# Retention followed by an MLP mixer on one core: masks that read two PSUM banks, seven quarter products for a third of batch 0, two crossbar turns, and order tables

## The chip, the core and the metric

The kernel runs on one core of a Trainium2 chip. TensorE (PE) multiplies matrices and puts the result in PSUM, which has eight banks here; VectorE (DVE) and ScalarE (ACT) read PSUM and SBUF and write either; GpSimd (POOL) and SyncE (SP) mostly issue transfers here, and the crossbar transposes go over SP's queue. Each engine works through its own list of instructions in order, and semaphores order the lists against one another. The metric is the device time in microseconds of one execution.

## What is computed

The first half is a retention (a linear attention whose state decays by a factor gamma of the head), the second a token and channel mixing MLP on its result. Sizes are B = 4 batches, H = 8 heads, S = 768 positions, D = 64; the mixer has 512 channels, 256 token features and 1536 channel features.

```
gamma = 1.0 - 2.0 ** (-5.0 - np.arange(H))
for t in range(S):
    state = gamma * state + outer(k[:, :, t], v[:, :, t])
    y[:, :, t] = q[:, :, t] @ state / sqrt(D)
x = y.transpose(0, 2, 1, 3).reshape(B, S, H * D)
h = relu(x.T @ w_tok1) @ w_tok2
u = x + h.T
out = u + relu(u @ w_ch1) @ w_ch2
```

## The kernel before

Line numbers are those of the kernel before. Inputs are cast to f16 and products are summed in f32 in PSUM.

`front(b, p)` does retention and token mixing for a pair p of heads of batch b, 16 pairs in all. The 768 positions are six chunks of 128. Keys and queries are scaled by powers of gamma (`decayed`, L577 and L579), and each is turned so that the 64 dimensions of both heads lie on the partitions (`turn`): by PE transposes (L610 and L612) with a copy out of PSUM (L621, L626), or by the crossbar over SP's queue (L598). `TURNS` gives a letter for k, q and u of each pair: t and w are turned by PE, x by the crossbar. In batches 0 and 1 the letters are "twt", in batches 2 and 3 "xxx". Then come the scores (`sc`, L700), 12 products of 128x128 for both heads and six chunks into four banks, two for each half of the sequence (one for each head); the masks (`am`, L707), four DVE instructions of 128x384 that multiply a bank by the causal mask into SBUF; the products with v (`av`, L728) into two banks Y; the state of each chunk (`st`, L649, with the copy `u0` at L659 and the links of the recurrence at L665), its scaled copy (L675, L677) and its product with the turned q (`y2`, L738) into the same Y. Copies take x out of Y (L750), `t1` (L764) and `t2` (L785) are the token mixing, again in two halves over the two banks Y, and further copies take u and X out (L750 as well). u is turned by PE transposes (`tru`, L824, with the copy at L830) or by the crossbar (L813).

`back(b)` does the channel mixing. The wide step multiplies u by w_ch1, 512 to 1536 channels: `widen` (L859) in plain products for batch 0, and `widen7` for the other three batches (L932), which cuts u and the weights into quarters and needs seven products of quarters in place of eight. That costs differences of u (`ts`, L904) and of the weights (`asum`, L1174), intermediate copies (`keep` and `seed`, L885), and an addition with relu on DVE (`joined`, L953) for two of the four results. A block `i` of `widen7` yields the row tiles i and i + 6 of the 12. The narrow step is `narrow7` (L1057), with sums of h (`sm`, L1035), the weights' differences `wsum` (L1161) and additions into X (L1071). `store` writes the result.

The order is planned when the program is built. `ORDERED` is a string of operation numbers and `WAYS` says for operations that DVE or ACT can do which of them does it. `arrange` goes through them with a model of each engine and of the DMA queues (`Rings`), and gives each PSUM use the bank that comes free first. Each such use is a tile of its own, named by its bank:

```
slot.tile = ps.tile(shape, dtype, name=f"bank{slot.at}", bufs=1)
```

In the opening, products of zeros (L1205) fill places where PE would stand.

Of the kernel before, what the change touches and what calls it, by code (L numbers as in the profile page):

```python
# [15 lines left out]

class Slot:


    def __init__(self, tag, good=0, need=0):  # L20
        self.tag, self.users, self.tile, self.at = tag, [], None, None
        self.good, self.need = good, need
# [3 lines left out]

# [16 lines left out]
class Rings:  # L43

    GEN = dict(SP=20.0, POOL=8.0, ACT=20.0)
    FIRST = dict(SP=600, POOL=1800, ACT=700)
    OPENING = dict(SP=1300, POOL=3000, ACT=700)
    LAND = dict(SP=900, ACT=900)  # L50
    DT = 40.0
    EARLY = 10000
    SOFT = (0.48, 0.52)
    HARD = (0.52, 0.43)
    LATER = (1400, 200)
    LATE = 100000
    PL = (1800, 2400, 2700)
    PT = (13500, 27000)

    def __init__(self):  # L60
        self.t = 0.0
        self.line = dict(SP=[], POOL=[], ACT=[])
        self.made = dict(SP=[0.0, 0.0, 0.0], POOL=[0.0, 0.0, 0.0], ACT=[0.0, 0.0, 0.0])

    def land(self, q, op, t):
        if q == "POOL":
            return self.PL[(t >= self.PT[0]) + (t >= self.PT[1])]
        return self.LAND[q] + (self.LATER[t >= self.LATE] if op.dma[0] == 48 else 0)

    def add(self, q, op, start):  # L70
        first = max(start + (self.OPENING if len(self.made[q]) == 3 else self.FIRST)[q], self.made[q][-1])
        end = first + op.dma[0] * self.GEN[q]
        self.made[q].append(end)
        self.line[q].append([op, float(op.dma[0]), first, end])

    def busy(self):
        return any(self.line.values())

    def step(self, landed):
        dt, t = self.DT, self.t  # L80
        on = [(q, l[0]) for q, l in self.line.items() if l and l[0][2] <= t]
        if on:
            hard = len(on) - ("POOL" in dict(on))
            late = t >= self.EARLY
            for q, x in on:
                share = (self.SOFT[late] if hard else 1.0) if q == "POOL" else (self.HARD[late] if hard < len(on) else 1.0) / hard
                n = share * dt / x[0].dma[1]
                if x[3] > t:
                    n = min(n, dt / self.GEN[q])
                x[1] -= n  # L90
                if x[1] <= 0:
                    self.line[q].pop(0)
                    landed.append((x[0], t + dt + self.land(q, x[0], t)))
        self.t = t + dt


SEM = 80
F_ON = 21000
FILL, F_NS, F_COLD = 0.7, 218, 320
BLOCK, ASKED, NEEDED, PE_0 = 256, -80, 192, 2  # L100
FETCH = (8200, 5000, 95000)
ENGINES = ("PE", "ACT", "DVE", "POOL", "SP")
SWITCH = {("", "wide"): 92, ("", "high"): 92, ("wide", ""): 100, ("high", ""): 111, ("wide", "high"): 105,
          ("high", "wide"): 105}
FREE = dict(PE=300, ACT=1150, DVE=1090, POOL=1200, SP=750)


def arrange(ops, BUFS, BANKS, seq, ways):


    INF = 1e18
    n = len(ops)
    end, start, eng = [None] * n, [None] * n, [None] * n
    begun = [False] * n
    rings = Rings()
    free = dict(FREE)
    bank_slot = {i: None for i in range(8)}
    buf_slot = {t: [None] * m for t, m in BUFS.items()}
    lanes, turns = [], []
    line = {e: [] for e in ENGINES}  # L120
    for i in seq:
        line[ops[i].ways[ways[i]][0]].append(ops[i])
    at = dict.fromkeys(ENGINES, 0)
    order = []
    landed = []
    tiled = ""
    count, pe_at, fetched = PE_0, 1100, {}
    t = 0.0

    def slot_free(s):  # L130
        m = 0
        for u in s.users:
            x = end[u.n]
            if x is None:
                return INF
            if x > m:
                m = x
        return m + SEM

    def ready(o, e):  # L140
        m = 0
        if o.behind is not None and not begun[o.behind.n]:
            return INF
        for d in o.after:
            x = end[d.n]
            if x is None:
                return INF
            if x > m:
                m = x
        for d in o.deps:  # L150
            if not begun[d.n]:
                return INF
            if end[d.n] is None:
                return INF
            if eng[d.n] == e and e == "PE":
                x = start[d.n]
            else:
                x = end[d.n] + (25 if eng[d.n] == e and d.dma is None else SEM) + o.guard
            if x > m:
                m = x  # L160
        return m

    def room(o):
        m, got = 0, []
        for s in o.takes:
            best = None
            held = bank_slot if s.tag in BANKS else buf_slot[s.tag]
            for i in BANKS[s.tag] if s.tag in BANKS else range(BUFS[s.tag]):
                if any(g[1] == i and (g[0].tag in BANKS if s.tag in BANKS else g[0].tag == s.tag) for g in got):
                    continue  # L170
                if s.tag in BANKS and i == 7 and t < F_ON:
                    continue
                if s.need and (held[i] is None or held[i].good < s.need):
                    continue
                x = 0 if held[i] is None else slot_free(held[i])
                if best is None or x < best[0]:
                    best = (x, i)
            if best is None or best[0] >= INF:
                return INF, None
            got.append((s, best[1]))  # L180
            m = max(m, best[0])
        return m, got

    def lane(o, e):
        if o.dma is None or e == "POOL" or len(lanes) < 8:
            return 0
        x = end[lanes[-8].n]
        if x is None:
            return INF
        x += SEM  # L190
        if o.dma[0] == 48 and len(turns) > 2:
            y = end[turns[-3].n]
            if y is None:
                return INF
            x = max(x, y - 900)
        return x

    left = n
    while left:
        moved = False  # L200
        wake = INF
        for e in ENGINES:
            if free[e] > t:
                wake = min(wake, free[e])
                continue
            if at[e] >= len(line[e]):
                continue
            o = line[e][at[e]]
            r = ready(o, e)
            if r > t:  # L210
                wake = min(wake, r)
                continue
            m, banks = room(o)
            m = max(m, lane(o, e))
            if m > t:
                wake = min(wake, m)
                continue
            at[e] += 1
            way = o.ways[ways[o.n]]
            s_ = t  # L220
            if e == "PE":
                if o.tiled != tiled:
                    s_ = max(t, free[e] + SWITCH[tiled, o.tiled])
                tiled = o.tiled
                o.fill = int((s_ - pe_at) * FILL / (F_NS if pe_at > 2000 else F_COLD)) if s_ < F_ON and s_ - pe_at > 400 else 0
                count += 2 * o.fill
                o.busy = way[1]
                for x in range(count - 2 * o.fill, count + o.ins):
                    if (x - ASKED) % BLOCK == 0:
                        fetched[(x - ASKED) // BLOCK] = s_ + max(0, x - count) * o.busy / o.ins + FETCH[s_ > FETCH[2]]  # L230
                    if (x - NEEDED) % BLOCK == 0 and x > NEEDED:
                        late = fetched.get((x - NEEDED) // BLOCK, 0) - (s_ + max(0, x - count) * o.busy / o.ins)
                        o.busy += max(0, late)
                count += o.ins
                pe_at = s_ + o.busy
            else:
                o.busy = way[1]
            start[o.n], eng[o.n], begun[o.n] = s_, e, True
            free[e] = s_ + o.busy
            if o.dma:  # L240
                rings.add(e, o, t)
                if e != "POOL":
                    lanes.append(o)
                    if o.dma[0] == 48:
                        turns.append(o)
                if e == "SP":
                    free[e] = max(t + way[1], rings.made["SP"][-3])
# [989 lines left out]
```

## Time and profile before

| | |
|---|---|
| median of 3 runs | 186.33 us (186.3 to 188.1) |
| span of the profiled execution (its time is not listed apart) | 185.2 us |
| PE clock granted in every stretch of the trace | 1.00 |
| DMA moved | 25.31 MB, mean 137 GB/s |
| masks (L707) | 64 instructions, 32.1 us of DVE |
| longest single wait of PE (L612, for the scaled k) | 1.7 us |

The rows of the profile stand with the prediction. A row of the groups reads: line, engine, operation, what it writes and from what, partitions x elements, count | busy us in all, mean ns of one | idle time of the engine just before them and what ended most of it. A row of the waits reads: engine and line, what it waited for: us in all, times, longest. A row of the chain reads: start, length, engine, tile and line. A DMA row ends with the median us from issue to landing.

### The profile page before, as it was taken

The page shows a single profiled execution, that of the slowest core. Times are in us where ns is not written, and L with a number is a line of the kernel's source. Part 1 is how long each engine was busy: PE and PEld are TensorE (multiplying, and loading weights), DVE is VectorE, ACT ScalarE, POOL GpSimd, SP SyncE. Part 2 cuts the span into 40 slices and gives each one's busy share as a digit, 9 for nine tenths or more (in the row PEclk, how much of TensorE's full clock was granted, in tenths as well). Part 3 has the DMA queues.
Part 4 walks back from the last instruction along what each step waited for, and adds up shares of the span by engine and source line. Part 5 has one row for each costly group of instructions (what it writes and reads, how often), then busy time and mean ns, then how long its engine had stood idle before and what let it go on. Part 6 is the DMA issues. An engine that isn't in the chain of part 4 may idle for free.

```text
span 185.2 us, 5235 instructions
## 1 busy us (share of the span) xinstructions
PE 176.4 (95%) x2077; PEld 133.9 (72%) x2077; DVE 166.9 (90%) x423; ACT 128.8 (70%) x299; POOL 52.7 (28%) x63
## 2 busy tenths in 40 slices
PE   7688999999999999999999999999999999999991
PEld 2345788666788998877568988966678986667881
DVE  3599989969999999998999999999999799779982
ACT  4587797594797998899997778798673425754220
POOL 7986548375363218540604000000000000000000
PEclk9999999999999999999999999999999999999999
DMA  5999999999999999999999989225132162510054
GB/s 179 195 153 179 182 199 207 174 182 207 161 157 154 93 157 100 156 153 125 168 134 107 155 182 244 72 42 108 23 113 48 57 212 100 186 57 2 4 202 140
DMA packets 92393, 25.31 MB, mean 137 GB/s; under 512 B 82000, under 2 KB 89552, under 8 KB 92368
## 3 DMA queue, kind: packets, MB, share of 16 engines
q0 software_dynamic: 67184, 12.78, 91.1%
q1 hardware_dynamic: 23600, 9.70, 25.9%
q10 hardware_dynamic: 1584, 2.49, 3.8%
q8 instruction: 16, 0.26, 0.6%
q14 instruction: 9, 0.07, 0.1%
HBM read 26.74 MB, written 6.29 MB: 178 GB/s over the span
## 4 chain that ended last, share of the span: by engine, by line
PE 85%; DVE 7%; DMA 4%; ACT 1%; SPq 0%; issue 0%; DVEq 0%; ACTq 0%
PE bank L1057 30%; PE bank L932 22%; PE bank L859 9%; PE bank L764 6%; PE bank L785 5%; DVE am L707 4%; DMA us<-in_k_dram 4%; PE bank L700 3%; PE bank L728 3%; PE bank L738 2%; PE bank L649 2%; PE bank L824 1%; DVE U L665 1%; DVE qT L621 1%; PE bank L612 1%; PE bank L610 1%
## 5 line engine op out<-in xcount | busy, mean ns | idle before, releaser
L707 DVE TENSOR_TENSOR am<-bank,mask 128x384 f16<-128x384 f32 x64 | 32.1, 546 | 0.4 <-PE bank L700 0.2
L885 ACT COPY us<-bank 128x384 f32<-128x384 f32 (+1 forms) x47 | 20.0, 434 | 16.5 <-PE bank L1057 14.0
L1057 PEld LDWEIGHTS <-hs 128*128 128x128 f16 x282 | 26.5, 98 | 3.6 <-DVE hs L1035 0.3
L880 ACT ACTIVATE h<-bank 128x384 f16<-128x384 f32 x49 | 23.4, 498 | 7.5 <-PE bank L859 3.9
L1057 PE MATMUL bank<-wsum,hs 128*128 128x256 f16 x216 | 27.9, 273 | 0.0
L932 PE MATMUL bank<-hs,late 128*128 128x384 f16 x108 | 23.3, 326 | 0.0
L1057 PEld LDWEIGHTS <-h 128*128 128x128 f16 x216 | 20.5, 98 | 3.0
L523 POOL DMA_DIRECT2D v<-in_v_dram x16 | 16.3, 1020 | 22.3 <-PE bank L728 12.2
L953 DVE CUSTOM_DVE_ANT_0 h<-bank,us 128x384 f16<-128x384 f32 x36 | 19.1, 550 | 2.3 <-PE bank L932 2.2
L1071 DVE TENSOR_TENSOR X<-X,bank 128x256 f32<-128x256 f32 (+1 forms) x49 | 19.3, 405 | 1.1 <-PE bank L1057 0.7
L1057 PE MATMUL bank<-wc,h 128*128 128x256 f16 x144 | 19.2, 273 | 0.0
L932 PEld LDWEIGHTS <-late 128*128 128x128 f16 x144 | 13.3, 98 | 7.8
L859 PE MATMUL bank<-uT,wc 128*128 128x384 f16 x96 | 17.9, 326 | 0.0
L523 POOL DMA_DIRECT2D k<-in_k_dram x15 | 15.4, 1031 | 7.7 <-ACT cross L675 2.0
L675 ACT ACTIVATE cross<-U,gp 64x320 f16<-64x320 f32 x27 | 15.1, 558 | 3.2 <-DVE U L665 2.9
L665 DVE SCALAR_TENSOR_TENSOR U<-U,gp,bank 128x64 f32<-128x64 f32 x64 | 16.8, 271 | 0.6
L885 ACT COPY bank<-bank 128x384 f32<-128x384 f32 (+1 forms) x28 | 12.1, 436 | 5.8 <-PE bank L932 3.4
L932 PE MATMUL bank<-uT,wc 128*128 128x384 f16 x72 | 15.8, 326 | 0.0
L785 PE MATMUL bank<-h,wt 128*128 128x128 f16 x192 | 14.3, 219 | 0.0
L750 ACT CAST x<-bank 128x384 f16<-128x384 f32 x27 | 12.2, 485 | 2.9 <-PE bank L738 2.6
L750 ACT COPY X<-bank 128x384 f32<-128x384 f32 x26 | 12.5, 493 | 1.8 <-PE bank L785 1.6
L932 PEld LDWEIGHTS <-wc 128*128 128x128 f16 x108 | 9.9, 98 | 5.1
(93 smaller groups left out, 342.6 us busy)
## 6 DMA issues: line engine op xcount, KB each, us to landing
out_dram<-X SPq DMA_DIRECT2D x13, 256.0 KB, 2.6
v<-in_v_dram POOLq DMA_DIRECT2D x16, 192.0 KB, 8.4
k<-in_k_dram POOLq DMA_DIRECT2D x15, 192.0 KB, 10.0
q<-in_q_dram POOLq DMA_DIRECT2D x14, 192.0 KB, 8.7
wc<-in_moe_w_ch_dram POOLq DMA_DIRECT2D x5, 512.0 KB, 13.1
out_dram<-X ACTq DMA_DIRECT2D x9, 256.0 KB, 2.1
hs<-in_q_dram SPq DMA_DIRECT2D x2, 384.0 KB, 3.6
wc<-in_moe_w_ch_dram POOLq DMA_DIRECT2D x2, 256.0 KB, 9.6
```

The lines of the kernel that those rows point to most:

```text
L523: (nc.sync if hard else nc.gpsimd).dma_start(out=tile_of(s, [P, 2, NC, D], FP if hard else F16), in_=src.rearrange("h (c p) d -> p (h c) d ...
L665: nc.vector.scalar_tensor_tensor(out=u[:, c], in0=u[:, c - 1], scalar=gp[:, p:p + 1], in1=chunk(c), op0=ALU.mult, op1=ALU.add)
L707: nc.vector.tensor_tensor(am, SC[g].tile[:, :m * P].rearrange("p (i t) -> p i t", t=P), (mask2[:, g // 2:g // 2 + 1] if paired else mask). ...
L750: (nc.scalar.copy if e == "ACT" else nc.vector.tensor_copy)(tile(), t)
L785: nc.tensor.matmul(Y[j].tile[:, 2 * i * D:2 * (i + 1) * D], wt2[:, jt, t], H1.tile[:, jt], start=False, stop=(jt == NJ - 1), skip_group_ch ...
L859: nc.tensor.matmul(acc[:, :SH], wc1[:, ct, ft * P:(ft + 1) * P], UT.tile[:, ct, sh * SH:(sh + 1) * SH], start=(ct == 0), stop=(ct == NP - 1))
L880: nc.scalar.activation(out, src, AF.Relu)
L885: (nc.scalar.copy if e == "ACT" else nc.vector.tensor_copy)(out, src)
L932: nc.tensor.matmul(acc[:, :SH], left(ct), r[:, ct], start=first and ct == 0, stop=ct == C2 - 1, skip_group_check=True)
L953: nc.vector._custom_dve(TENSOR_ADD_SAT, out=h(m, sh), in0=R.tile[:, :SH], in1=KS.tile[:, j], s0=BIG, s1=0.0)
L1057: nc.tensor.matmul(acc[:, lo], l[:, j], r[:, j], start=first and j == 0, stop=j == K2 - 1, skip_group_check=True)
L1071: nc.vector.tensor_tensor(dst(), dst(), b_(), ALU.add)
```

## The change

PSUM becomes one tile of eight banks. A slot is a slice of it; where two banks are to be read by one instruction, `two` takes them as one view with a stride:

```diff
+    psum = ps.tile([P, 8, 512], FP, name="psum")
...
-            slot.tile = ps.tile(shape, dtype, name=f"bank{slot.at}", bufs=1)
+            slot.tile = psum[:, slot.at]
+            if dtype != FP:
+                slot.tile = slot.tile.bitcast(dtype)
...
+    def two(a, b):
+        lo, hi = sorted((a.at, b.at))
+        both = psum[:, lo:hi + 1:hi - lo]
+        a.tile, b.tile = both[:, 0], both[:, 1]
+        return both
```

The masks take both heads of a half of the sequence at once: two instructions of 128x768 for a pair in place of four of 128x384. The buffers of their results are four of the double size in place of eight. `av` waits for one mask where it waited for two.

```diff
+        for hf in range(2):
+            def emit(hf=hf):
+                am = tile_of(AM[hf], [P, 2, HC, P], F16)
+                nc.vector.tensor_tensor(am, pairs[hf][:, :, :SH].rearrange("p j (i t) -> p j i t", t=P),
+                                        mask.unsqueeze(1).to_broadcast([P, 2, HC, P]), ALU.mult)
+            am_ops.append(op(one("DVE", dve(2 * SH), emit), [sc, mask_op], [AM[hf]], SC[2 * hf:2 * hf + 2], key="am"))
```

In batch 0, row tiles 0 to 3 and 6 to 9 of the wide step stay plain, and blocks 4 and 5 go by `widen7`; u of pairs 2 and 3 of batch 1 is turned by the crossbar. `widen` and `widen7` take lists of tiles and blocks for that.

```diff
+OPT = dict(wide7=(1, 2, 3), mix=4, turned=(), whole=0, held='qQk', turns='twt twt twt twt twt twt twx twx xxx xxx xxx xxx xxx xxx xxx xxx')
...
-        def widen(sh):
+        def widen(sh, tiles):
...
-            for ft in range(NF):
+            for ft in tiles:
...
-        def widen7():
+        def widen7(blocks):
...
-            for i in range(M2):
+            for i in blocks:
                 block(i)
```

One of the four differences of w_ch2 is written over a quarter of w_ch2 that is not needed afterwards:

```diff
-    wsum = const_p.tile([P, 4, K2, N2], F16, name="wsum")
+    wsum = const_p.tile([P, 3, K2, N2], F16, name="wsum")
+
+    def wpart(j):
+        return wc2[:, :K2, N2:] if j == 2 else wsum[:, j - (j == 3)]
```

An unused branch for pairs of a different layout goes, and with it two masks (L455), two tables of decays and their index, that the old kernel still prepared. `Rings` and `arrange` go: the order, the engine of each operation and, new, the bank or buffer of each slot are read from tables, and so is the place of the fills.

```diff
+PLACES = (
+    "0010100011210130021230124561002103124151603202223064210125010062134351024010021735311276350320267120",
...
+def place(ops, BUFS, BANKS):
+    digit = {c: i for i, c in enumerate(DIGITS)}
+    text = "".join(ORDERED)
+    seq = [ops[digit[a] * 62 + digit[c]] for a, c in zip(text[::2], text[1::2])]
+    at = iter("".join(PLACES))
+    for o in seq:
+        for s in o.takes:
+            s.at = digit[next(at)]
+    for n, fill in FILLS:
+        ops[n].fill = fill
+    ways = "".join(WAYS)
+    return [(o, o.ways[digit[ways[o.n]]]) for o in seq]
```

In the built order the change shows as follows. A row gives the line, the operation, what it writes and from what, and in brackets the engines or queues whose semaphores it waits for. In the new kernel all banks are named psum; the bank numbers told below are those of the table of places.

The masks of batch 2, pair 2, on DVE, before: each reads one bank and waits for PE alone.

```order
L885 COPY us_1983<-bank_1906 128x384 [waits DVE_49,PE_49]
L707 TENSOR_TENSOR am_2019<-bank_1987,mask 128x384 [waits PE_49]
L707 TENSOR_TENSOR am_2025<-bank_1985,mask 128x384
L707 TENSOR_TENSOR am_2033<-bank_1988,mask 128x384 [waits PE_49]
L707 TENSOR_TENSOR am_2041<-bank_1986,mask 128x384
L665 SCALAR_TENSOR_TENSOR U_2038<-U_2038,gp,bank_2005 128x64 [waits PE_49,Activation_49]
```

The same masks on DVE now. The first reads banks 0 and 3 and the second banks 5 and 6:

```order
L494 COPY X_1682<-psum 128x3x128 [waits PE_49]
L630 TENSOR_SCALAR h_1586<-psum 128x384 [waits PE_49]
L494 COPY X_1682<-psum 128x3x128 [waits PE_49]
L464 TENSOR_TENSOR am_1810<-psum,mask 128x768 [waits PE_49,Activation_49]
L464 TENSOR_TENSOR am_1817<-psum,mask 128x768
L431 SCALAR_TENSOR_TENSOR U_1819<-U_1819,gp,psum 128x64 [waits Activation_49]
```

Four rows have become two, and the first of them waits for ACT too. On PE, what follows the scores and the state products of that pair, before:

```order
L649 LDWEIGHTS k_1640
L649 MATMUL bank_2005<-v_1267,k_1640 64x64
L932 LDWEIGHTS late_851
L932 MATMUL bank_1942<-hs_1692,late_851 128x384 [waits Activation_49]
L932 LDWEIGHTS late_851
L932 MATMUL bank_1942<-hs_1692,late_851 128x384
L932 LDWEIGHTS late_851
L932 MATMUL bank_1906<-hs_1692,late_851 128x384 [waits DVE_49]
```

And now, where the first product (weights "late", the differences of w_ch1) goes to bank 1 and the second (weights "wc") to bank 2:

```order
L416 LDWEIGHTS k_1670
L416 MATMUL psum<-v_1529,k_1670 64x64
L680 LDWEIGHTS late_749
L680 MATMUL psum<-hs_1516,late_749 128x384 [waits Activation_49]
L680 LDWEIGHTS late_749
L680 MATMUL psum<-hs_1516,late_749 128x384
L680 LDWEIGHTS wc_84
L680 MATMUL psum<-uT_1112,wc_84 128x384 [waits DVE_49]
```

The place of the products is alike, but the DVE instruction that the last row waits for is now the first mask. The second place is the opening: DVE at the masks of pairs 1 and 2 of batch 0, before.

```order
L707 TENSOR_TENSOR am_311<-bank_288,mask 128x384 [waits PE_49]
L707 TENSOR_TENSOR am_325<-bank_289,mask 128x384 [waits PE_49]
L665 SCALAR_TENSOR_TENSOR U_269<-U_269,gp,bank_249 128x64 [waits DVE_49]
L707 TENSOR_TENSOR am_337<-bank_286,mask 128x384
L665 SCALAR_TENSOR_TENSOR U_339<-U_339,gp,bank_314 128x64 [waits Activation_49]
L707 TENSOR_TENSOR am_362<-bank_287,mask 128x384
L665 SCALAR_TENSOR_TENSOR U_339<-U_339,gp,bank_314 128x64 [waits DVE_49]
```

And now, with pair 1's masks (banks 0 and 6, then 1 and 5) and pair 2's (0 and 6, then 2 and 4):

```order
L431 SCALAR_TENSOR_TENSOR U_273<-U_273,gp,psum 128x64 [waits DVE_49]
L464 TENSOR_TENSOR am_299<-psum,mask 128x768 [waits PE_49]
L431 SCALAR_TENSOR_TENSOR U_273<-U_273,gp,psum 128x64 [waits DVE_49]
L464 TENSOR_TENSOR am_314<-psum,mask 128x768 [waits Activation_49]
L464 TENSOR_TENSOR am_335<-psum,mask 128x768 [waits PE_49]
L464 TENSOR_TENSOR am_361<-psum,mask 128x768 [waits PE_49,Activation_49]
L431 SCALAR_TENSOR_TENSOR U_375<-U_375,gp,psum 128x64 [waits Activation_49]
```

The links of U that stood between the masks have moved, and the second mask of each pair waits for ACT.

More of the change, by code (lines that the diff above doesn't have):

```diff
@@ L40, in __init__ @@
         ops.append(self)
[L43 to L94, printed above, removed]
@@ L97 @@
[L97 to L247, printed above, removed]
-            else:
-                end[o.n] = s_ + way[2] + o.busy - way[1]
-            for s, i in banks:
-                (bank_slot if s.tag in BANKS else buf_slot[s.tag])[i] = s
-            order.append((o, e, way, banks))
-            left -= 1
-            moved = True
-            wake = min(wake, free[e])
-        if moved:
-            continue
-        nxt = wake
-        while rings.busy() and rings.t < nxt:
-            rings.step(landed)
-            for o, x in landed:
-                end[o.n] = x
-                nxt = min(nxt, max(x, t + 1))
-            landed.clear()
-        if not rings.busy():
-            rings.t = max(rings.t, min(nxt, t + 40))
-        if nxt >= INF:
-            raise RuntimeError(f"the plan is stuck at {t}: {left} left")
-        t = max(nxt, t + 1) if nxt <= t else nxt
-    while rings.busy():
-        rings.step(landed)
-    for o, x in landed:
-        end[o.n] = x
-    for o, e, way, banks in order:
-        for s, i in banks:
-            s.at = i
-    return max(x for x in end), order, start, end
@@ L454 @@
     since_op = prep("since", "POOL", 450, emit, takes=[SINCE])
-    mask2_ops = [prep("mask2", "DVE", 200, lambda t=t: nc.vector.tensor_scalar(
-        mask2[:, t], SINCE.tile[:, 0], back2[:, t:t + 1], 0.0, ALU.add, ALU.is_ge), [since_op, back2_op], uses=[SINCE]) for t in range(2)]
     gq_ops = []
@@ L533, in load @@
         else:
-            o = request((-20, 0, b, p), 710 if wide else 850 if (b, p) in PAIRED and what != "q" else 1030, emit, dma, [s], key=("load", b, p, what))
+            o = request((-20, 0, b, p), 710 if wide else 1030, emit, dma, [s], key=("load", b, p, what))
         loads[b, p, what] = (s, o)
     def front(b, p):
-        first, paired = b == 0, (b, p) in PAIRED
+        first = b == 0
         FA = "first" if first else "front"
@@ L602, in turn @@
             T = Slot(FA)
-            split = mode == "w" and (b, p, "q") not in HARD
+            split = mode == "w" and (b, p, "q") not in HARD and not OPT["whole"]
             def emit():
@@ L679, in front @@
                          [RS, US] if j else [US], behind=rs[0] if j else None, key="rs"))
-        lots = [[(j, hf + 2 * i if paired else hf * HC + i) for i in range(HC)] for hf in range(2) for j in range(2)]
-        AM, SC = [Slot("am") for _ in lots], [Slot(FA, good=2) for _ in lots]
-        place = {x: (g, i) for g, lot in enumerate(lots) for i, x in enumerate(lot)}
-        am_ops = []
+        AM, SC = [Slot("am") for _ in range(2)], [Slot(FA, good=2) for _ in range(4)]
+        am_ops, pairs = [], {}
@@ L702, in front @@
-        sc = op(one("PE", (430, 585) if paired else (330, 485), emit), [kt, qt], SC, [KT, QT], tiled="high", key="sc")
-        sc.guard = RESERVE[0] if TURN[b, p, "q"] == "x" else sc.guard
-        for g, lot in enumerate(lots):
-            def emit(g=g, m=len(lot)):
-                am = tile_of(AM[g], [P, m, P], F16)
-                nc.vector.tensor_tensor(am, SC[g].tile[:, :m * P].rearrange("p (i t) -> p i t", t=P),
-                                        (mask2[:, g // 2:g // 2 + 1] if paired else mask).to_broadcast([P, m, P]), ALU.mult)
-            am_ops.append(op(one("DVE", dve(len(lot) * P), emit), [sc, mask2_ops[g // 2] if paired else mask_op], [AM[g]], [SC[g]],
-                             key="am"))
+            for hf in range(2):
+                pairs[hf] = two(SC[2 * hf], SC[2 * hf + 1])
@@ new lines, in emit @@
+            for c in range(NC):
+                for j in range(2):
+                    hf, i = c // HC, c % HC
+                    rows, t = rows_of(j), slice(c * P, (c + 1) * P)
+                    nc.tensor.matmul(SC[2 * hf + j].tile[:, i * P:(i + 1) * P], KT.tile[rows, t], QT.tile[rows, t],
+                                     start=(i == 0), stop=True, skip_group_check=True)
+        sc = op(one("PE", (330, 485), emit), [kt, qt], SC, [KT, QT], tiled="high", key="sc")
+        sc.guard = RESERVE[0] if TURN[b, p, "q"] == "x" else sc.guard
```

299 lines of the change are left out of this document (106 added, 193 removed).

## Prediction

> **What bounds the kernel now.** I read the head of the page first: span, busy time by engine, PE's row over 40 slices, and the share of each engine in the chain that ended last.
>
> ```profile
> span 185.2 us, 5235 instructions
> PE 176.4 (95%) x2077; PEld 133.9 (72%) x2077; DVE 166.9 (90%) x423; ACT 128.8 (70%) x299; POOL 52.7 (28%) x63
> PE   7688999999999999999999999999999999999991
> PE 85%; DVE 7%; DMA 4%; ACT 1%; SPq 0%; issue 0%; DVEq 0%; ACTq 0%
> ```
>
> PE carries 85% of the chain and is nearly full from the seventh slice on; DVE is close behind at 90%. So the second view is the busy time by stage: the opening, two stretches in which the retention of later batches runs beside the MLP of earlier ones, and the tail.
>
> ```profile
> core 0: us, PE busy (x) PEld busy (x) DVE busy (x) ACT busy (x) POOL busy (x), PEclk, DMA share, GB/s
> 0.00:31.00 31.00, 25.96 (x378) 17.10 (x379) 25.16 (x86) 22.29 (x45) 22.86 (x33) 1.00 1.72 184
> 31.00:60.00 29.00, 29.00 (x339) 20.87 (x337) 26.61 (x55) 21.42 (x53) 14.53 (x16) 1.00 2.04 175
> 60.00:135.00 75.00, 74.99 (x948) 59.03 (x946) 72.77 (x190) 64.32 (x153) 15.27 (x15) 1.00 1.30 125
> 135.00:181.50 46.50, 46.49 (x420) 36.88 (x419) 41.50 (x91) 20.72 (x51) 0.00 (x0) 1.00 0.30 102
> ```
>
> From 31 us to the end PE is never idle, so there one us more or less of PE, work or wait, is one us of the end. DVE has 29.00 - 26.61 = 2.4 us free in the second stretch and 75.00 - 72.77 = 2.2 us in the third: little cover for anything that makes it wait. Next I looked at what PE waits for, and at the chain inside the opening.
>
> ```profile
> PE bank L612 <- ACT k L577: 1.7, 1, 1.7
> ...
> PE bank L728 <- DVE am L707: 0.5, 2, 0.3
> ```
>
> ```profile
> 10.75 0.97 DVE qT L621
> 11.73 1.49 DVE am L707 x3
> 13.22 0.19 DVE U L665
> ...
> 18.23 0.93 DVE am L707 x2
> 19.16 0.88 DVE qT L621
> ...
> 27.01 1.87 DVE am L707 x4
> ```
>
> From 10.75 to 20 us the chain is DVE back to back, masks (L707) above all: there a us of DVE is a us of the end. After that PE has hardly ever waited for a mask: 0.5 us in the whole run.
>
> **The change part by part.** *PE work.* A third of batch 0's plain products (L859; 32 of the 96 there) become 28 products of quarters of the same shape, so 4 of 128x384 go. Two pairs of batch 1 lose six transposes each (L824). The prices are from the chain, where PE runs back to back:
>
> ```profile
> 77.40 0.33 PE bank L824 x6
> ...
> 146.16 7.86 PE bank L1057 x72
> 154.02 10.72 PE bank L932 x66
> ```
>
> A 128x384 product takes 10.72 / 66 = 0.162 us, four of them 0.65; twelve transposes take 2 x 0.33 = 0.66. Together -1.3 us, all on the path. The six fills that also go stand where PE waits anyway: nothing.
>
> *Masks.* 64 instructions of 128x384 become 32 of 128x768. DVE's other work changes too:
>
> ```profile
> L707 DVE TENSOR_TENSOR am<-bank,mask 128x384 f16<-128x384 f32 x64 | 32.1, 546 | 0.4 <-PE bank L700 0.2
> L621 DVE TENSOR_TENSOR qT<-bank,X 128x768 f16<-128x768 f16 x8 | 7.4, 942 | 1.6 <-PE bank L610 1.6
> L953 DVE CUSTOM_DVE_ANT_0 h<-bank,us 128x384 f16<-128x384 f32 x36 | 19.1, 550 | 2.3 <-PE bank L932 2.2
> L904 DVE TENSOR_TENSOR hs<-uT,hs 128x768 f16<-128x768 f16 x6 | 3.3, 547 | 0.0
> L455 DVE TENSOR_SCALAR mask<-us,back 128x128 f32<-128x128 f32 x2 | 0.8, 422 | 0.0
> ```
>
> Back to back, a mask costs 1.87 / 4 = 0.47 us. The trace has no 128x768 mask; the nearest row is the scaling out of PSUM in the same shape, 0.88 us in the chain (19.16), and twice the old price is 0.94. I take 0.88, as that row differs only in its type. A pair of heads then costs 1.76 in place of 1.87: -0.11 each, -1.8 over 16 pairs. Against this stand four joins (L953) and four differences (L904) more, 8 x 0.55 = +4.4, two preparations less (L455), -0.8, and decays and copies that move between DVE and ACT and cancel but for some tenths. DVE gains 2 us of work in all, most of the joins and differences in the second stretch, which has 2.4 free: hidden, but with nothing left.
>
> *What a mask now waits for.* This is the part that the list of edits does not show. Before, each bank was a tile of its own. Now PSUM is one tile, and a mask reads two banks of it with a stride. In the built order the masks wait for ACT in 14 cases of 32, where before none of 64 did. Followed back, these are copies and products in banks that lie between the two that the mask reads: a stride from bank 0 to bank 3 is ordered as if banks 1 and 2 were read too. By the table of places 21 of the 32 masks have banks between theirs. Such an order also holds among readers, as the trace shows for single banks:
>
> ```profile
> DVE u L750 <- ACT X L750: 0.3, 1, 0.3
> ...
> ACT X L750 <- DVE u L750: 0.2, 1, 0.2
> ```
>
> The Trainium skill, page "PSUM — Partial Sum Buffer", section "PSUM bank collisions raise a hardware error", says that two engines must not touch one bank at once, reads against reads included, and that accesses to different banks may run in parallel. The two rows above agree for the one bank. By that rule the banks between need no order at all, and the sum would be -1.3 and -0.9 against 186.3, or 184.1; the kernel waits nevertheless, since its semaphores do.
>
> *The price in the opening* (batch 0). Three rows more:
>
> ```profile
> L626 ACT COPY kT<-bank 128x768 f16<-128x768 f16 x4 | 3.2, 799 | 1.2 <-PE bank L612 1.2
> L750 ACT CAST x<-bank 128x384 f16<-128x384 f32 x27 | 12.2, 485 | 2.9 <-PE bank L738 2.6
> ```
>
> Pair 1: its first mask reads banks 0 and 6. The transposes of the next k go to bank 2 and wait for it, ACT's copy of them follows, and the second mask (banks 1 and 5) waits for that copy: 0.33 + 0.80, less the 0.19 of a link of U that DVE has meanwhile, is +0.94. Pair 2: ACT's copy out of bank 3 waits for the first mask (0 and 6), and the second (2 and 4) for the copy: +0.48. Pairs 0 and 3 have one such copy each that may or may not have ended: 0 to 0.48 each, half taken, +0.5. Saved there are 4 x 0.11 by longer masks and one preparation on the path, 0.42: -0.9. Sum +1.1, between -0.9 if no copy is late, and +2 if all are and the preparation was hidden.
>
> *The price after 31 us.* Here PE issues in order, so a PE instruction that waits for a mask holds everything behind it. Ten PE instructions wait for a mask in whose banks they have no part, while that mask waits for the PE instruction ahead. In two places nothing stands between. Batch 2 pair 2: the first mask (banks 0 and 3) waits for a product into bank 1, and PE's next product, into bank 2, waits for the mask. Batch 3 pair 3: the mask of banks 1 and 7 waits for the first half of t2 (bank 3), the second half (bank 4) waits for the mask. Each time PE stands for a mask, 0.88, and two handovers of a tenth or less: 1.0, together 2.0. In the other eight PE has work of its own between, which I add up from the order at 0.162 a product and 0.33 for six transposes: 0.65, 0.65, 1.0, 1.0, 0.8, 0.43, 0.5 and 1.0. What is left of 1.0 is 0.35, 0.35, 0, 0, 0.2, 0.57, 0.5 and 0: 2.0 us. Sum +4.0; at least 0 if DVE is never in step with PE there, at most 10 x 1.1 = 11 if DVE is late at each.
>
> *Crossbar.* The two pairs' u goes over SP's queue as eight others do:
>
> ```profile
> uT<-u SPq DMA_TRANSPOSE x8, 3.6
> ```
>
> PE's first product that needs them comes some 6 us of PE work after the issue: hidden, and SP's other transposes are not on the chain.
>
> *Sum.* The profiled execution's span is 185.2; its time is not given beside it, and the median of the runs lies 1.1 above the span, which I take as what lies around it. -1.3 + 1.1 + 4.0 = +3.8, so 185.2 + 3.8 + 1.1 = 190.1 us.
>
> **The rivals.** *Most waits fall into slack.* Only the two bare places cost anything, as masks that come earlier than I think leave the eight covered, and the opening's waits lie beside PE's waits for loads (1.7 at L612): -1.3 + 2.0 = +0.7, 187.0. For it speaks that PE is idle for 5 us in the opening; against it that the chain there is DVE's from 10.75 on.
>
> *No added wait costs anything, and the kernel is faster.* If each mask that waits is reached by DVE only after the copy or product in question is done, -1.3 and -0.9 stand alone: 184.1. It is decided at the masks themselves: DVE would have to be a us or more behind PE at each of the ten places. DVE's 97% of the third stretch speaks for it, the 0.5 us that PE waited for masks before against it, since then PE did not depend on that lag.
>
> *DVE becomes the bound.* While a mask waits for PE or ACT, DVE does nothing else. The eight covered places alone hold it for the 6.0 us of the covers, with 2 us more of work and 4.6 free in the second and third stretch: +3.4 of DVE on its own, which in places comes on top of PE's waits. With all of it 193.5. Against it: part of these stretches would be the same wait seen twice.
>
> *The change doesn't do what it says:* if the long mask costs more than two short ones, DVE loses instead of gaining. At 1.0 us each, +2 over the run, this is the last rival again.
>
> **How the numbers follow.** A measurement of this kernel can tell about 1% from no change, 1.9 us. Forecast 190.1: 0.46. Slack, 187.0: 0.27, within 1%. No cost, 184.1: 0.17, faster by over 1%. DVE bound, 193.5: 0.10. So faster 0.17, same 0.27, slower 0.56. The forecast's own range is 188.1 to 192.5, from its eight covered places at nothing to the opening at its upper bound and half a us more at each of three places. The range that leaves out 2 in 10 reaches from 184.1, with half of the no-cost case below it, to 193.2, with half of the DVE case above.
>
> **What would show it.** PE's waits would list products (L608 and L680 of the new file), t2 (L532) and copies waiting for the mask L464, 3 to 5 us in sum where the old page has 0.5; masks would wait for ACT in the opening, 1 to 2 us in sum; a mask would take 0.88 to 0.97 us. PE's busy time would be 1.3 us less but for its waits. I am wrong if PE waits for masks for less than 1.5 us in all, or if DVE shows no idle time ahead of L464.

## The result, and the profile after

The changed kernel takes 197.26 us (median of 4 runs, 196.32 to 197.81) where the kernel before took 186.5 beside it: a ratio of 1.0542, 95% interval 1.047 to 1.0615, so some 10 us slower. The forecast was 190.1 us and its range ended at 193.2: the direction was right, the size was not.

The profiled execution of the changed kernel, the fastest of its four, has a span 9.3 us longer than that of the kernel before. First the head of its page, with the same rows as before:

```profile
span 194.5 us, 5201 instructions
...
PE 177.9 (91%) x2055; PEld 134.1 (69%) x2055; DVE 171.1 (88%) x397; ACT 127.6 (66%) x297; POOL 52.1 (27%) x61
...
PE   7667798999998999899789999999979999999992
...
PE 66%; DVE 18%; DMA 6%; ACT 5%; issue 2%; DVEq 0%; SPq 0%; ACTq 0%
```

No engine is fuller than it was; each has a lower share of a longer span. PE's part of the chain fell from 85% to 66%, and DVE's rose from 7% to 18%. The work hands over between engines more often. That share doesn't measure the loss, though: in the first experiment below, which has no loss, it is 65% for PE and 21% for DVE. The busy time by stage, in the columns of the prediction's table, puts numbers to it:

```profile
0.00:31.00 31.00, 24.14 (x317) 15.57 (x318) 23.09 (x72) 19.09 (x39) 22.32 (x31) 0.94 1.59 186
31.00:60.00 29.00, 27.74 (x340) 19.80 (x339) 27.86 (x53) 24.26 (x56) 12.58 (x13) 1.00 1.86 165
60.00:135.00 75.00, 71.31 (x916) 56.49 (x913) 68.70 (x165) 59.39 (x144) 17.17 (x17) 1.00 1.31 135
```

In the third stretch PE and DVE, which had 0.0 and 2.2 us free before, have 3.7 and 6.3 us free. Of DVE's 6.3 us, 3.0 lie just ahead of masks. What PE waits for:

```profile
PE psum L475 <- DVE am L464: 2.5, 3, 1.1
PE psum L680 <- DVE am L464: 1.9, 2, 1.1
PE psum L912 <- DVE zero L909: 1.2, 1, 1.2
PE psum L532 <- DVE am L464: 1.1, 1, 1.1
PE psum L387 <- DVE am L464: 1.0, 1, 1.0
...
PE psum L778 <- ACT us L633: 0.8, 1, 0.8
...
PE psum L570 <- DVE am L464: 0.5, 1, 0.5
...
PE psum L608 <- DVE am L464: 0.3, 1, 0.3
```

The masks (L464) hold PE for 7.5 us in all, with 0.2 us in rows not shown; before it was 0.5. Only L475, the product with v, reads what a mask writes. The transposes (L387, L570), the wide products (L608, L680) and t2 (L532) have no data in common with one. The group of the masks shows the other side:

```profile
L464 DVE TENSOR_TENSOR am<-psum,mask 128x768 f16<-128x768 f32 x32 | 29.8, 951 | 7.1 <-ACT kT L401 1.5
```

DVE stands idle for 7.1 us just ahead of its masks, where it was 0.4. The longest piece is for a copy of a turned k, which that mask does not read. One of the bare places, batch 2 pair 2, on the timeline of PE and then of DVE:

```profile
94.28 0.50 PE L680 MATMUL psum<-hs,late 128*128 128x384 f16 x2
95.90 0.48 PE L680 MATMUL psum<-uT,wc 128*128 128x384 f16 x2 [1.12 <-DVE am L464]
```

```profile
94.89 1.82 DVE L464 TENSOR_TENSOR am<-psum,mask 128x768 f16<-128x768 f32 x2 [0.77 <-PE psum L680]
```

DVE waits 0.77 us until PE's product into bank 1 has ended, then PE waits 1.12 us for the mask before it may write bank 2, while the mask reads banks 0 and 3.

To see where the 9.3 us come in, I took the start of an instruction on PE less all the work that PE had done by then. The work is counted from start to start at full clock: 0.163 us for 128x384, 0.109 for 128x256, 0.056 for 128x128, 0.028 and 0.016 for the small ones, fills left out. The difference is the lag, and two kernels with other orders can be compared by it at the same place of the program. The last column is the first experiment below.

| start of | before | after | all masks split |
|---|---|---|---|
| first t1 | 15.3 | 18.3 | 14.5 |
| batch 0's first wide product | 17.3 | 20.1 | 16.3 |
| scores of batch 2, pair 0 | 19.4 | 23.3 | 18.5 |
| scores of batch 2, pair 2 | 20.3 | 25.6 | 20.7 |
| scores of batch 3, pair 0 | 20.9 | 29.2 | 21.9 |
| scores of batch 3, pair 3 | 21.9 | 31.3 | 23.1 |
| last products | 21.9 | 32.6 | 23.6 |

After the change the lag is 2.8 us more at batch 0's wide step and 10.7 more at the end; 1.3 us less work make 9.4 of it.

### The profile page after: what moved, and what is told of

Its sections match the earlier page's. It is cut to its first block, busy times and chain, and to the rows that moved or that the text cites. A ratio compares the mean times of both kernels' runs of the same rounds, so it can differ in the third digit from the quotient of the medians.

```text
span 194.5 us, 5201 instructions
## 1 busy us (share of the span) xinstructions
PE 177.9 (91%) x2055; PEld 134.1 (69%) x2055; DVE 171.1 (88%) x397; ACT 127.6 (66%) x297; POOL 52.1 (27%) x61
## 4 chain that ended last, share of the span: by engine, by line
PE 66%; DVE 18%; DMA 6%; ACT 5%; issue 2%; DVEq 0%; SPq 0%; ACTq 0%
PE psum L778 22%; PE psum L680 20%; DVE am L464 6%; PE psum L511 4%; PE psum L532 4%; PE psum L608 4%; DMA uT<-u 4%; PE psum L475 3%; DVE U L431 2%; PE psum L485 2%; DMA hs<-in_q_dram 2%; PE psum L457 2%; PE psum L387 2%; DVE X L792 1%; PE psum L570 1%
## 5 line engine op out<-in xcount | busy, mean ns | idle before, releaser
L464 DVE TENSOR_TENSOR am<-psum,mask 128x768 f16<-128x768 f32 x32 | 29.8, 951 | 7.1 <-ACT kT L401 1.5
L633 ACT COPY us<-psum 128x384 f32<-128x384 f32 (+1 forms) x49 | 21.3, 443 | 18.7 <-PE psum L778 14.4
L628 ACT ACTIVATE h<-psum 128x384 f16<-128x384 f32 x44 | 20.6, 498 | 9.9 <-PE psum L680 6.4
L309 POOL DMA_DIRECT2D v<-in_v_dram x16 | 16.3, 1022 | 39.0 <-PE psum L485 19.4
L680 PE MATMUL psum<-hs,late 128*128 128x384 f16 x120 | 25.7, 326 | 0.8 <-DVE am L464 0.7
L701 DVE CUSTOM_DVE_ANT_0 h<-psum,us 128x384 f16<-128x384 f32 x40 | 21.0, 551 | 2.6 <-PE psum L680 1.6
L680 PEld LDWEIGHTS <-late 128*128 128x128 f16 x160 | 14.9, 98 | 9.9 <-issue 1.2
L792 DVE TENSOR_TENSOR X<-X,psum 128x256 f32<-128x256 f32 (+1 forms) x49 | 19.1, 408 | 1.7 <-PE psum L778 1.3
L680 PE MATMUL psum<-uT,wc 128*128 128x384 f16 x80 | 18.6, 326 | 1.4 <-DVE am L464 1.1
L778 PE MATMUL psum<-wc,h 128*128 128x256 f16 x144 | 19.3, 273 | 0.0
L778 PE MATMUL psum<-wsum,hs 128*128 128x256 f16 x144 | 19.3, 273 | 0.0
L778 PE MATMUL psum<-wc,hs 128*128 128x256 f16 x138 | 18.3, 273 | 0.8 <-ACT us L633 0.8
L680 PEld LDWEIGHTS <-wc 128*128 128x128 f16 x120 | 11.2, 98 | 8.0 <-issue 2.1
L532 PE MATMUL psum<-h,wt 128*128 128x128 f16 x192 | 14.5, 219 | 1.1 <-DVE am L464 1.1
```

Of the source, the lines that this page charges most:

```text
L309: (nc.sync if hard else nc.gpsimd).dma_start(out=tile_of(s, [P, 2, NC, D], FP if hard else F16), in_=src.rearrange("h (c p) d -> p (h c) d ...
L464: nc.vector.tensor_tensor(am, pairs[hf][:, :, :SH].rearrange("p j (i t) -> p j i t", t=P), mask.unsqueeze(1).to_broadcast([P, 2, HC, P]), ...
L532: nc.tensor.matmul(Y[j].tile[:, 2 * i * D:2 * (i + 1) * D], wt2[:, jt, t], H1.tile[:, jt], start=False, stop=(jt == NJ - 1), skip_group_ch ...
L628: nc.scalar.activation(out, src, AF.Relu)
L633: (nc.scalar.copy if e == "ACT" else nc.vector.tensor_copy)(out, src)
L680: nc.tensor.matmul(acc[:, :SH], left(ct), r[:, ct], start=first and ct == 0, stop=ct == C2 - 1, skip_group_check=True)
```

## The experiments

Two theories stood against each other. "Banks between": a mask that strides over two banks is ordered against every instruction on the banks between them, and these waits are the loss. "The new order": the tables, batch 0's quarter products or the crossbar turns make it. Ratios are to the kernel before on the same chip, and 0.01 is 1.9 us.

**All masks split.** Order, engines and banks stay, each long mask is issued as two of one bank each:

```diff
             def emit(hf=hf):
                 am = tile_of(AM[hf], [P, 2, HC, P], F16)
+                for j in range(2):
+                    nc.vector.tensor_tensor(am[:, j], SC[2 * hf + j].tile[:, :SH].rearrange("p (i t) -> p i t", t=P),
+                                            mask.to_broadcast([P, HC, P]), ALU.mult)
+                return
```

> The new kernel with each long mask issued as two masks of 128x384, one bank each, at the same place of the order, on the same engine, with the same banks; nothing else differs. Theory 'banks between' (a mask that strides over two banks is ordered against every instruction on the banks between, and that is the loss): PE's waits for masks fall from 7.5 us to under 1.5 us and the time from 197.3 to between 185.5 and 189 us, about that of the kernel before, although DVE has 1.8 us more of masks. Rival 'the new order' (the table itself, batch 0's quarter products and the crossbar turns make the loss): 194 to 198 us.

Measured: ratio 1.0011 (0.9981 to 1.004), median 187.36 beside 187.4. The group of the masks in that run (L466 is the mask's line there):

```profile
L466 DVE TENSOR_TENSOR am<-psum,mask 128x384 f16<-128x384 f32 x64 | 31.4, 547 | 0.2
```

DVE has 1.6 us more of masks and 6.9 us less idle time ahead of them, and the whole loss is gone. So the loss is in the long masks. PE's 1.3 us of saved work are not seen either, which is taken up below.

**Only batch 0's masks split, and only the others.** The same edit under `if b == 0` and under `if b > 0`.

> As the run with all masks split, but only the masks of batch 0 are split. The lag behind the work that PE has done was 3.0 us more than before at the start of the first token mixing and 2.7 us at the start of batch 0's wide step. Theory 'banks between': that part goes, 194 to 195.5 us, and PE's clock in the slice at 15 to 19 us is back at 0.9 or more. Rival 'the new order': 196.5 to 198 us, since the opening's lag comes from fewer fills and moved loads.

> As the run with all masks split, but only the masks of batches 1 to 3 are split. Theory 'banks between': the lag that grows after 31 us (7.9 us more than before) goes, 188.5 to 191 us, and the sum of this gain and that of batch 0 alone is within 1 us of the gain with all split. Rival 'the new order': within 1.5 us of 197.3, as the order after 31 us waits for the joins and differences of the quarter products instead.

Measured: 1.0283 (1.024 to 1.0325) for batch 0 alone and 1.0251 (1.0179 to 1.0324) for the rest. From 1.0542 that is a gain of 4.8 us and of 5.4 us; together 10.2, and all split gave 9.9. The two parts add up, as expected. Both expectations missed on the sizes: the opening is worth more than the lag of one trace said, and the rest less, since 2.7 us of the lag that grows after batch 0's first wide product is there with all masks split too (16.3 to 23.6, where before it was 17.3 to 21.9). PE's granted clock goes with the opening's long masks: its mean over an execution was 0.996 or more in all four with batch 0's masks split, 0.973 to 0.990 in the four with only the others split, and 0.982 to 0.991 in the four of the changed kernel.

**The banks renamed.** Each bank number is mapped to another throughout, so every true dependence stays, and only what lies between two banks changes:

```diff
+PERM = (0, 2, 5, 6, 1, 4, 7, 3)
...
             s.at = digit[next(at)]
+            if s.tag in BANKS:
+                s.at = PERM[s.at]
...
-            nc.tensor.matmul(psum[:, 7], zero[:, :P], zero, start=True, stop=True)
+            nc.tensor.matmul(psum[:, PERM[7]], zero[:, :P], zero, start=True, stop=True)
```

The other renaming is (1, 5, 0, 2, 3, 4, 6, 7).

> The new kernel with its eight bank numbers renamed throughout, so that each instruction has the same partners in its bank as before, but 30 of the 32 masks have banks between theirs (21 in the new kernel) and waits between instructions without a common bank are about 80 where the new kernel has 44. Long masks stay. Theory 'banks between': 203 to 214 us, the loss of 11 us over the old kernel growing in proportion to these waits. Rival 'the new order': 197.3 within 1.5 us, since no true dependence changes.

> The new kernel with its bank numbers renamed throughout so that 14 of 32 masks have banks between theirs (21 in the new kernel, 30 in the far renaming) and the waits between instructions without a common bank are 24 where the new kernel has 44 and the far renaming 80. Long masks stay, and so does every true dependence. Theory 'banks between': the loss shrinks with the number of these waits, from 10.2 us at 44 to about 5.5 us at 24, so 191 to 193 us, ratio to the kernel before 1.02 to 1.04. Rival 'a few places carry the loss, whatever the count': the ratio stays at 1.045 or more, or falls under 1.015.

Measured: 1.131 (1.1257 to 1.1364) with the far names and 1.0341 (1.0284 to 1.0398) with the near ones. Nothing but names differs between these two and the changed kernel, so neither the order nor the length of a mask makes this difference. Counted in the built programs, the waits between instructions without a common bank are 0 with all masks split, 24 with the near names, 44 in the changed kernel and 80 with the far names; the loss is 0.2, 6.4, 10.1 and 24.4 us. The loss rises with the count, at 0.23 to 0.31 us for each such wait.

**Long masks where the banks are neighbours.** The split stands under `if abs(SC[2 * hf].at - SC[2 * hf + 1].at) > 1`.

> The new kernel with the 21 long masks that have banks between theirs split into two of 128x384, and the 11 whose banks are neighbours left long. Theory 'banks between': the 11 long masks cost nothing but their own 0.87 us and save DVE 11 x 0.06 = 0.7 us, so the time is that of all split or up to 0.7 us less: ratio to the kernel before 0.995 to 1.003. Rival 'a long mask itself holds its two banks too long': each of the 11 makes scores or products wait for the bank that it would have freed half a mask sooner, 0.45 us each at most, ratio 1.005 to 1.025.

Measured: 0.9959 (0.9934 to 0.9983). Its two groups of masks (L466 the short, L469 the long ones):

```profile
L466 DVE TENSOR_TENSOR am<-psum,mask 128x384 f16<-128x384 f32 x42 | 20.9, 550 | 0.1
...
L469 DVE TENSOR_TENSOR am<-psum,mask 128x768 f16<-128x768 f32 x11 | 10.5, 951 | 0.1
```

A long mask of two neighbours has hardly any idle time ahead of it, and PE waits for one only at a product with v that reads it (0.3 us). This version is the fastest so far: its whole interval lies below the kernel before, by 0.8 us or 0.4% in the middle.

**The two bare places.** Only the masks of banks 0 and 3 (batch 2 pair 2) and of banks 1 and 7 (batch 3 pair 3) split.

> The new kernel with two masks split only: the ones at the two bare places of the prediction (batch 2 pair 2, banks 0 and 3; batch 3 pair 3, banks 1 and 7). The prediction priced each at 1.0 us; the trace of the new kernel has PE standing 1.28 us at each. If waits add up: 2.0 to 2.8 us less, ratio to the kernel before 1.039 to 1.044. Rival 'the waits move': PE stands at the next of these waits instead, ratio 1.050 to 1.056.

Measured: 1.0485 (1.044 to 1.0529), 1.1 us less, though this interval overlaps that of the changed kernel. Of the 2.2 us that PE stood there, half came back in the end. The clock blurs this: its mean was 0.971 to 0.982 in the four executions here, against 0.982 to 0.991, and the profiled one had two stretches of 3.4 us at 0.50 in the opening where the changed kernel's had one. The growth of the lag after batch 0's wide step leaves the opening out: it is 12.5 us in the changed kernel and 11.3 in this one. At the first place its growth falls from 2.0 to 0.8 us; at the second from 1.3 to 0.9 only, as PE then stands for a copy of ACT (0.8 us, in both).

**The masks alone, in the old order.** The kernel before, with PSUM as one tile; the first of a pair's two masks in its order becomes a long one, the second goes.

```diff
+                if hf in waiting:
+                    return
+                waiting[hf] = free_masks.pop(0)
+                x, y = SC[2 * hf], SC[2 * hf + 1]
+                at = sorted((x.at, y.at))
+                both = psum[:, at[0]:at[1] + 1:at[1] - at[0]][:, :, :SH].rearrange("p j (i t) -> p j i t", t=P)
...
+                nc.vector.tensor_tensor(am, both, mask.unsqueeze(1).to_broadcast([P, 2, HC, P]), ALU.mult)
```

A first version put it where the later mask stood:

> The kernel before, with its order, its engines and its banks, with PSUM as one tile and each pair of masks of a half of the sequence joined into one of 128x768 that stands where the later of the two stood. No quarter products in batch 0, no crossbar turns in batch 1, no tables. Some 40 of its waits are between instructions without a common bank (44 in the new kernel). Theory 'banks between': 194 to 199 us, about as slow as the new kernel. Rival 'the new order': 185 to 188 us, as the masks alone take 1.8 us off DVE.

There the bank of the earlier one may have been given on already, so that version masks other numbers; it measured 1.1028 (1.0962 to 1.1094). The second version:

> The kernel before, with its order, its engines and its banks, with PSUM as one tile and each pair of masks of a half of the sequence joined into one of 128x768, this time standing where the earlier of the two stood, and with four buffers that are handed on only when the products with v have read them. No quarter products in batch 0, no crossbar turns in batch 1, no tables. Some 46 of its waits are between instructions without a common bank. Theory 'banks between': 196 to 207 us. Rival 'the new order makes the loss': 185 to 188 us, as the masks alone take 1.8 us off VectorE.

Measured: 1.1002 (1.0913 to 1.109). The masks alone cost the old order 18.7 us, more than the whole change costs. There too 21 of the 32 masks have banks between, but of 46 such waits, against 44, each costs more: the count alone doesn't set the price. In that version the order and the mask buffers were not planned for long masks either, and no run takes these parts from the 18.7 us. The tables of the changed kernel do better than the old order with long masks, and still lose.

**The opening's two pairs.** Only the four masks of pairs 1 and 2 of batch 0 split.

> The new kernel with only the four long masks of pairs 1 and 2 of batch 0 split. The prediction priced the waits there at 0.94 + 0.48 = 1.4 us; in the trace of the new kernel VectorE stands 1.53 us ahead of pair 1's second mask and 0.82 + 0.55 us ahead of pair 2's two, 2.9 us in all. If these idle times are what the opening costs: 2.9 us less, 193.7 to 195 us, ratio to the kernel before 1.035 to 1.043. Rival 'the waits move to pairs 0 and 3': at most 1 us less, ratio 1.048 or more.

Measured: 1.0347 (1.0285 to 1.0409), 3.6 us less. The idle time of DVE at these masks is 2.9 of it. The rest may be PE's clock, which no run separates. Busy time in three pieces of the opening of the changed kernel, and in the last of them in this run:

```profile
10.00:15.00 5.00, 3.47 (x70) 2.48 (x72) 4.46 (x8) 1.29 (x5) 4.53 (x6) 1.00 2.08 171
15.00:17.50 2.50, 1.47 (x20) 0.85 (x15) 2.25 (x8) 0.96 (x2) 1.01 (x3) 0.87 1.51 193
17.50:20.00 2.50, 2.33 (x19) 1.06 (x17) 0.96 (x1) 1.98 (x4) 1.23 (x2) 0.50 2.34 164
```

```profile
17.50:20.00 2.50, 2.38 (x57) 1.98 (x56) 2.46 (x7) 2.44 (x8) 1.40 (x2) 1.00 2.32 160
```

The granted clock fell to 0.50 in the changed kernel; with pairs 1 and 2 split it stays at 1.00 in the trace. The pieces hold other instructions, so their counts can't be compared. The same ones can: six transposes of k and three products of zeros in the changed kernel, then with all masks split, where the clock is 1.00.

```profile
17.12 0.80 PE L387 MATMUL psum<-ident,k 128*128 128x128 f16 x6 [1.03 <-DVE am L464]
17.71 1.49 PE L912 MATMUL psum<-zero 128*128 128x512 f16 x3
```

```profile
15.61 0.50 PE L387 MATMUL psum<-ident,k 128*128 128x128 f16 x6 [0.52 <-DVE k L351]
15.94 0.81 PE L917 MATMUL psum<-zero 128*128 128x512 f16 x3
```

**The crossbar.** With all masks split, the two turns of batch 1 replaced by zeros from GpSimd:

```diff
             def emit():
                 if UT.tile is None:
                     tile_of(UT, [P, NP, S], F16)
+                if b == 1:
+                    return nc.gpsimd.memset(UT.tile[:, p], 0.0)
                 nc.sync.dma_start_transpose(out=UT.tile[:, p].rearrange("d (c t) -> d c t", t=P),
```

> The run with all masks split, in which the two crossbar turns of u of batch 1 are replaced by GpSimd filling that part with zeros, so batch 1's channel mixing works on other numbers and the transposes are left out. In the run with all masks split the lag behind PE's work grows by 1.8 us where batch 1's wide step begins, 0.9 us of it a named wait for the crossbar's landing, against 0.5 us before. Theory 'the crossbar lands late': 1.0 to 1.8 us less than with all masks split, ratio to the kernel before 0.990 to 0.995. Rival 'VectorE is the bound there': the ratio stays at 1.000, within 0.3%.

Measured: 0.9973 (0.9947 to 0.9999), 0.7 us less than with all split and not the 1.0 to 1.8 expected, and the two intervals overlap. The traces agree: with all masks split PE waits for the landing, and that row is absent here. The row, and the piece of that run's chain that ends in it:

```profile
PE psum L685 <- DMA uT<-u: 0.9, 1, 0.9
```

```profile
72.10 7.64 DMA uT<-u
79.74 0.04 issue
79.78 0.65 PE psum L685 x3
```

The transfer took 7.64 us from issue to landing. Last, an attempt to win this back in the version with neighbours long: u of pair 3 turned by PE into bank 6, which is empty there, with the copy on ACT.

> The run that splits only the masks with banks between theirs, in which u of pair 3 of batch 1 is turned by six PE transposes into bank 6 while that bank is empty and copied by ScalarE, instead of by the crossbar. PE gains 0.33 us of work, ScalarE 0.80 us. Theory 'the crossbar lands late': the wait of 0.5 to 0.9 us for its landing goes, 0.2 to 0.7 us less in all, ratio to the kernel before 0.992 to 0.995. Rival 'PE pays what the wait gave back': ratio 0.996 to 1.000.

Measured: 0.9957 (0.9928 to 0.9986), the same as without it. The wait for the landing, 0.5 us without this edit, is gone from the trace. That PE pays what the wait gave back would fit, but both theories have values inside the interval, so it is not shown.

## Why the prediction fell short

Step by step, by its own terms; the sum was +3.8 us, and the trace has +9.3.

- **PE work, -1.3.** Right: summed from the records at the prices given above, PE's work is 159.3 us before and 157.9 after. PE's busy time did not show it, as it rose from 176.4 to 177.9 us; with all masks split it is 174.6. With all masks split nothing of the gain is left in the time, as other things took it back (below).
- **The cause.** Waits between instructions that share no bank: right, and settled by the renaming, which changes nothing else. One reading behind it was too wide: of the 14 masks of the changed kernel that wait for ACT, ten do so for a bank between theirs and four for an earlier use of a bank of their own; with all masks split 14 short masks wait for ACT too.
- **After 31 us, +4.0.** Named waits of PE for masks that do not feed it are 2.2 at the bare places (2.0 forecast) and 0.8 + 0.5 + 0.3 at others, with 0.3 for a product with v; the eight were put at 2.0. Sum 4.1. To this comes the 0.8 us for ACT's copy. By lag, the masks cost 12.5 - 7.3 = 5.2 us after batch 0's wide step, and by the timed run 5.4. Here mechanism and size were nearly right, though the places don't simply add up: two of them returned 1.1 of 2.2 us.
- **The opening, +1.1. This is the step that failed most.** By lag it came to 18.3 - 15.3 = 3.0 at the first t1. Its savings were 0.9, of which 0.42 had nothing to do with longer masks; with all masks split, so without longer masks, the lag at the first t1 is 14.5 against 15.3 before, 0.8 less. Its waits were put at 0.94 + 0.48 + 0.5 = 1.9 us, less 0.44 by longer masks: 1.5. By lag the long masks cost 18.3 - 14.5 = 3.8, by the timed run 4.8. The chain of the changed kernel shows how:

```profile
16.20 0.88 DVE am L464
17.07 0.04 issue
17.12 0.81 PE psum L387 x6
17.93 0.02 issue
17.95 0.81 ACT kT L401
18.76 0.02 issue
18.78 0.97 DVE am L464
19.75 0.04 issue
19.80 0.50 PE psum L457 x6
20.30 0.24 PE psum L485 x2
20.54 0.02 issue
20.57 0.97 DVE am L464
21.53 0.04 issue
21.57 0.34 PE psum L475 x6
```

The loop of mask, k transposes, copy and mask is there as forecast, but the six transposes took 0.81 us, not the 0.33 of a row at 77 us, where PE ran back to back. They take 0.50 standing alone at full clock (with all masks split, above), and the other 0.3 fit the halved clock. So DVE stood 1.53 us and not 0.94. Between pair 2's masks I had counted one copy, 0.48. In fact its first mask also waits for PE, whose next scores wait for the mask before and whose y2 comes behind them (0.82 us of DVE idle), and its second waits 0.55. Pair 0's share came as taken: 0.28 + 0.22 us. In all 3.4 us of idle time instead of 1.9.
- **What was left out: the clock.** The price of PE work was taken at full clock. In the changed kernel it did not stay there: from 13.40 to 16.85 us PE was busy for 1.88 of 3.45 us, and the clock was 0.50 in the next piece.

```profile
13.40:16.85 3.45, 1.88 (x31) 1.09 (x31) 2.91 (x10) 2.10 (x5) 2.32 (x3) 1.00 1.68 189
16.85:20.20 3.35, 2.92 (x21) 1.47 (x20) 1.36 (x3) 2.18 (x4) 1.52 (x2) 0.50 2.18 169
```

With all masks split PE was busy for 2.77 us of that same first stretch, and its clock stayed at 1.00. That a lower clock goes with the long masks of batch 0 is shown by the two partial splits above, though means of 0.987 to 0.989 also occur without long masks, in three of ten executions with all masks split. How little work it takes is not shown: the kernel before was busy for only 1.73 us of 3.40 in an earlier stretch, 51%, and kept its clock.

```profile
7.40:10.80 3.40, 1.73 (x23) 0.91 (x21) 2.22 (x7) 3.13 (x6) 3.40 (x5) 1.00 2.48 157
```

A stretch of 3.4 us at half clock costs at most 1.7 us, by an estimate from its length. Means of 0.982 and 0.983 in two of the changed kernel's other executions would be two such stretches, so the trace shows less of this loss than the median has. The Trainium skill, page "TensorE: Matmul & The Clock Gate", section "Part 1: The HAM clock gate (the "warmup" mystery)", says that the clock has two states, half and full, and drops to half after an idle window of about 3.4 us. The half rate agrees with the 0.50 here. The idle window does not, if PE has to stand still in it: the longest stretch in which PE stood before it was 1.14 us, and the busy share was 54%.
- **The crossbar, hidden.** Wrong by 0.7 us where the masks no longer delay PE. I took the median landing, 3.6 us, against a cover of 6; this one took 7.64. In the changed kernel itself PE came so late that it waited 0.2 us only.
- **"Hidden, but with nothing left", VectorE's 2 us.** The sum put this at nothing, and that failed too, by 2.7 us with the crossbar in it. With all masks split, and so without a single such wait, the lag still grows by 7.3 us from batch 0's wide step to the end, where it grew by 4.6 before. The crossbar is 0.7 of these 2.7 us. What the other 2.0 are, more joins and differences on DVE or the order itself, no run separates; it stays open.

Of the rivals, the one without cost fell, as did the one of slack. VectorE as the bound fell too: of its 6.3 us of idle time in the third stretch only 3.0 lie ahead of masks, so it was not full apart from them. The account of the trace, with the forecast behind each term, is: -1.3 work (-1.3), -1.0 by a better opening apart from masks (-0.4), +3.8 masks in the opening (+1.5), +5.2 masks after it (+4.0), +2.7 the rest of the new order (0): +9.4, with 9.3 measured and 3.8 forecast.

## What to carry to other kernels

An instruction that strides over parts of a shared tile may be ordered against everything between them: after such a change compare who waits for whom in the built order, and let long accesses cover neighbours only. Price a loop of waits by every hop in it, and at the clock that PE has in that place, since PE that waits much may also lose its clock. If a cause depends on names alone, renaming is the cleanest experiment: it changes nothing else.

## What the runs showed of the hardware that was not expected

PE's granted clock fell to 0.50 after a stretch of 3.45 us in which PE was busy 54% of the time and never stood for more than 1.14 us, and stayed at 1.00 where it was busy 80% of the same stretch (2.77 us). It also stayed at 1.00 in the kernel before after 3.40 us with 51%, so the busy share of the profile alone doesn't tell when it falls. A mask over two banks took 0.95 us whether its banks were neighbours or six apart (0.937 to 0.959 for all 32), so the distance of the banks itself cost nothing. One crossbar transpose of 128x768 took 7.64 us to land, where the median of the ten is 3.0.
